# Attention scores as one burst of 64-row matmuls a block, two heads at once in the halves of the array, in a shared ring of four PSUM banks, with q unpadded and new costs in the planner

## The chip, the cores and the metric

One core of a Trainium2 chip. The metric is the device time of one execution in microseconds (us). Times of a kernel are medians of its executions; an execution counts as slow when it is over 1.5% above the fastest of its kernel, and the ratios leave it out. They are computed as said under the result. TensorE is PE, VectorE DVE, ScalarE ACT, GpSimd POOL, SyncE SP.

## The reference

Sliding-window attention with linear distance biases over 8 x 8 heads of 576 tokens, then a two-layer block with a squared ReLU:

```python
B, H, S, D = 8, 8, 576, 64
scores = (q @ k.T) / sqrt(D) - slope[h] * |i - j|      # only where 0 <= i - j < 128
attn   = softmax(scores)
x      = (attn @ v) as [B*S, H*D]                      # 4608 x 512
h      = x @ w_in                                      # 512 x 2048
out    = relu(h)**2 @ w_out                            # 2048 x 512
```

## The kernel before

Everything is planned at build time: each piece of work is a task with an estimated cost on its engine, a due date (`key`), and slots of rings that it takes and gives back. A list scheduler walks through them, always takes the task that can start first, and so fixes the order of every engine's instructions. The estimates are not times of the chip; if they are wrong, the order is wrong, and an engine in its fixed order stands and waits (below, PE for 1.54 us at a score and DVE for 4.31 us at a copy).

A sequence is five blocks of tokens (four of 128, one of 64), so there are 40 blocks. For each block the kernel needs q and k transposed, the scores for this block and the one before it (two "parts"), the exponential on ACT, the mask on DVE, pv, the normalisation on DVE, and the result transposed into `xT`. From the third sequence on, transposes are DMAs on SP's queue. The large matmuls of 512 columns ("h" and "o") fill PE in between; group g of h needs xT of 512 tokens.

```python
plan = Plan({"h": 2, "o": 2, "s": 2, "att": 2, ...})       # PSUM banks by ring
due = (b * S + kb * 128 + n) / 4 - 192 - 150               # in large matmuls
...
# from the third sequence on:
t_k = plan.add({"SP": 100.0}, due - 80, turn_k, ..., dma=500.0)    # DMA transpose of k
t_t = plan.add({"SP": 100.0}, due - 80, turn_q, ..., dma=500.0)    # of q
for c2 in range(2):                                        # DVE: spread q's two heads,
    nc.vector.tensor_copy(qp[po:po + 64, :, c2, 0:n],      # the other half of the rows
                          qT[po:po + 64, :, 0:n])          # is zero
...
for c in range(4):                                         # two heads a matmul
    for part, mk in parts:                                 # 128 rows, 2n columns
        nc.tensor.matmul(slot_s[:, :, part, 0:n], kT[mk][:, c, :],
                         qp[:, c, :, 0:n], start=True, stop=True)
    # each c: its own bank, own exponential (ACT) and mask (DVE)
```

The softmax here doesn't subtract the row's maximum and nothing guards it: scores larger than these inputs give would overflow.

## Time and profile before

| | before |
|---|---|
| median of runs | 333.6 to 334.7 us in the sets below |
| span of the profile | 333.0 us |
| first large matmul (h) | 27.08 us |
| PE busy | 308.0 us, 92% |
| score matmuls | 288, all 128 x 128 |

The waits of PE in the middle stall are these two and five shorter ones (from PE's timeline; in brackets the idle time before the row and what ended it):

```profile
88.89 0.39 PE L364 MATMUL ps_s<-qp_92,kT_88 128*128 128x256 bf16 x2 [1.54 <-DMA kT_88<-kn_74]
102.09 0.28 PE L364 MATMUL ps_s<-qp_92,kT_86 128*128 128x256 bf16 x1 [1.53 <-DVE qp_92 L320]
```

The five others end at transposes of k too; the second one shown ends at DVE's copy of q, which had itself waited 1.66 us for the transpose of q. One thing about reading the lines: records are lost. The page counts 554 of 576 matmuls of h and 560 of 576 of o. A lost record leaves a hole of exactly one matmul (0.216 us). Where I sum holes from starts below, holes of that size after 27 us are left out as lost records. For the kernel before, the sum gives 13.3 us before 27 us, 2.5 between 27 and 57, 0.4 between 57 and 83, 7.3 between 83 and 126, and nothing after that.

### The profile page before, as it was taken

How to read it: one execution, taken by the hardware profiler on the slowest of the kernel's cores; microseconds unless marked ns; L12 is line 12 of the kernel's file. 1: busy time of each engine (PE TensorE's matmuls, PEld its weight loads, DVE VectorE, ACT ScalarE, POOL GpSimd, SP SyncE). 2: the span in 40 equal slices, each digit the busy share in tenths (PEclk: the TensorE clock that was granted, in tenths of full speed). 3: DMA queues.
4: the chain of work that ended last, by engine and by line, in shares of the span. 5: the costliest groups of instructions: out<-in, count | busy, mean ns of one | idle time of the engine just before them, and what ended most of it. 6: DMA issues, size and time to landing. Idle time of an engine off the chain costs nothing.

```text
span 333.0 us, 5942 instructions
## 1 busy us (share of the span) xinstructions
PE 308.0 (92%) x2098; PEld 164.8 (49%) x2136; DVE 182.3 (55%) x570; ACT 186.2 (56%) x362; POOL 107.4 (32%) x133
## 2 busy tenths in 40 slices
PE   1679999999887899999999999999999999999995
PEld 1555566446454555555555555555554444444442
DVE  6676797349676776665666655755554222222200
ACT  4595785558575565656565566655574344443411
POOL 8976757153473555363422521100000000000000
PEclk9999999999999999999999999999999999999999
DMA  9999999999999999999999999653112001000021
GB/s 73 140 200 168 171 199 149 161 148 143 133 180 160 165 177 214 163 181 181 169 130 115 139 157 117 100 89 66 47 50 56 31 33 61 34 33 31 31 94 63
DMA packets 169373, 39.58 MB, mean 119 GB/s; under 512 B 160640, under 2 KB 164736, under 8 KB 169344
## 3 DMA queue, kind: packets, MB, share of 16 engines
q0 software_dynamic: 116736, 18.36, 89.0%
q1 hardware_dynamic: 52608, 20.85, 34.0%
q8 instruction: 16, 0.26, 0.3%
q14 instruction: 13, 0.11, 0.1%
HBM read 36.70 MB, written 9.44 MB: 139 GB/s over the span
## 4 chain that ended last, share of the span: by engine, by line
PE 79%; DMA 9%; DVE 5%; ACT 4%; issue 1%; ACTq 0%
PE o L511 34%; PE h L482 33%; PE ps_s L364 7%; DMA kT_87<-kn_73 5%; DMA kT_85<-kn_71 4%; PE pv L405 4%; PE tp L332 1%; DVE P_95 L390 1%; ACT masks L221 1%; ACT qp_93 L293 1%; ACT P_97 L382 1%; PE xp L450 0%; ACT P_95 L382 0%; DVE g L496 0%; DVE x_100 L431 0%
## 5 line engine op out<-in xcount | busy, mean ns | idle before, releaser
L482 PE MATMUL h<-xT,w_in_sb 128*128 128x512 bf16 x554 | 152.6, 379 | 0.8
L511 PE MATMUL o<-w_out_sb,g 128*128 128x512 bf16 x560 | 151.7, 379 | 0.8
L490 ACT ACTIVATE rt<-h 128x512 bf16<-128x512 f32 x144 | 85.6, 597 | 83.9 <-PE h L482 78.5
L496 DVE TENSOR_TENSOR g<-rt 128x512 bf16<-128x512 bf16 x144 | 60.4, 420 | 70.3 <-ACT rt L490 68.9
L511 PEld LDWEIGHTS <-g 128*128 128x128 bf16 x576 | 54.6, 98 | 52.2
L482 PEld LDWEIGHTS <-w_in_sb 128*128 128x128 bf16 x576 | 54.8, 98 | 49.7 <-issue 0.2
L382 ACT ACTIVATE P_95<-ps_s 128x512 bf16<-128x512 f32 (+1 forms) x56 | 27.0, 507 | 12.4 <-PE ps_s L364 12.1
L522 ACT ACTIVATE osb<-o 128x512 f32<-128x512 f32 x36 | 21.5, 598 | 19.8 <-PE o L511 16.6
L382 ACT ACTIVATE P_96<-ps_s 128x512 bf16<-128x512 f32 (+1 forms) x52 | 25.9, 517 | 10.5 <-PE ps_s L364 10.0
L382 ACT ACTIVATE P_97<-ps_s 128x512 bf16<-128x512 f32 (+1 forms) x52 | 25.7, 516 | 7.3 <-PE ps_s L364 7.1
L390 DVE TENSOR_TENSOR P_95<-P_95,masks 128x512 bf16<-128x512 bf16 (+1 forms) x56 | 20.1, 364 | 13.5 <-ACT P_95 L382 12.8
L390 DVE TENSOR_TENSOR P_96<-P_96,masks 128x512 bf16<-128x512 bf16 (+1 forms) x52 | 18.9, 368 | 10.3 <-ACT P_96 L382 9.4
L426 DVE RECIPROCAL rec<-pv 128x4 f32<-128x4 f32 (+1 forms) x80 | 13.8, 176 | 16.7 <-PE pv L405 16.3
L390 DVE TENSOR_TENSOR P_97<-P_97,masks 128x512 bf16<-128x512 bf16 (+1 forms) x52 | 18.8, 367 | 7.3 <-ACT P_97 L382 6.6
L273 POOL DMA_DIRECT2D kn_74<-in_k_dram x10 | 8.5, 845 | 25.2 <-DMA kT_88<-kn_74 8.7
L273 POOL DMA_DIRECT2D kn_73<-in_k_dram x10 | 8.5, 847 | 22.9 <-DMA kT_87<-kn_73 21.1
L405 PEld LDWEIGHTS <-P_95 128*128 128x128 bf16 x200 | 10.2, 99 | 5.1 <-DVE P_95 L390 0.3
L364 PEld LDWEIGHTS <-kT_88 128*128 128x128 bf16 x72 | 6.9, 98 | 11.0 <-DMA kT_88<-kn_74 3.0
L364 PEld LDWEIGHTS <-kT_86 128*128 128x128 bf16 x72 | 7.1, 99 | 10.4 <-issue 2.6
L431 DVE TENSOR_TENSOR x_98<-pv,rec 128x256 bf16<-128x256 f32 (+1 forms) x28 | 11.7, 418 | 0.4
L273 POOL DMA_DIRECT2D qn_77<-in_q_dram x10 | 8.5, 847 | 10.1 <-DMA qT_89<-qn_77 3.8
L364 PEld LDWEIGHTS <-kT_85 128*128 128x128 bf16 x72 | 7.2, 101 | 8.7 <-issue 1.6
(107 smaller groups left out, 327.9 us busy)
## 6 DMA issues: line engine op xcount, KB each, us to landing
out_dram<-osb SPq DMA_DIRECT2D x36, 256.0 KB, 2.3
w_in_sb<-in_moe_w_in_dram POOLq DMA_DIRECT2D x4, 512.0 KB, 8.9
w_out_sb<-in_moe_w_out_dram POOLq DMA_DIRECT2D x4, 512.0 KB, 10.5
kn_71<-in_k_dram POOLq DMA_DIRECT2D x8, 128.0 KB, 6.4
qn_75<-in_q_dram POOLq DMA_DIRECT2D x8, 128.0 KB, 6.3
kn_72<-in_k_dram POOLq DMA_DIRECT2D x8, 128.0 KB, 7.4
qn_76<-in_q_dram POOLq DMA_DIRECT2D x8, 128.0 KB, 7.8
kn_73<-in_k_dram POOLq DMA_DIRECT2D x8, 128.0 KB, 6.5
```

What stands on the lines that cost most here:

```text
L273: nc.gpsimd.dma_start(o, src[b, :, kb * 128:kb * 128 + n, :].rearrange("h s d -> s h d"))
L364: nc.tensor.matmul(slot_s.tile.rearrange("p (c t q) -> p c t q", c=2, t=2)[:, :, part, 0:n], kT[sk_of[mk].idx][:, c, :], qp[sq.idx][:, c, ...
L382: nc.scalar.activation(view(Pt[sP.idx][:, 2 * c:2 * c + 2]), view(slot_s.tile.rearrange("p (c t q) -> p c t q", c=2, t=2)), AF.Exp, bias=0 ...
L390: nc.vector.tensor_tensor(pt, pt, view(masks[:, 2 * c:2 * c + 2]), op=ALU.mult)
L405: nc.tensor.matmul(slot_v.tile[:, hi * (D + 1):(hi + 1) * (D + 1)], Pt[sP.idx][:, h, part, :], vt[s_in[mk, "v"].idx][:, h, :], start=part ...
L426: nc.vector.reciprocal(srec.tile[0:n, :], pv[0:n, :, D])
L431: nc.vector.tensor_tensor(xt[sx.idx][0:n, hf * 256:(hf + 1) * 256].rearrange("p (h e) -> p h e", h=4), pv[0:n, :, 0:D], srec.tile[0:n, :]. ...
L482: nc.tensor.matmul(slot.tile, w_in_sb[:, cc, fc * 128:(fc + 1) * 128], xT[:, cc, g * 512:(g + 1) * 512], start=cc == 0, stop=cc == C - 1)
L490: nc.scalar.activation(srt.tile, slot.tile, AF.Relu, bias=0.0, scale=1.0)
L496: nc.vector.tensor_tensor(sg.tile[:, fc, :], srt.tile, srt.tile, op=ALU.mult)
L511: nc.tensor.matmul(slot.tile, sg.tile[:, fc, t * 128:(t + 1) * 128], w_out_sb[:, fc, :], start=fc == 0, stop=fc == FCB - 1)
L522: nc.scalar.activation(so.tile, slot.tile, AF.Copy)
```

## The change

It means to halve PE's work on scores. The heads are 64 wide, so a matmul for one head uses only 64 of the array's 128 rows (the trace of the changed kernel notes 64*128 for it, that of the kernel before 128*128 throughout). Before, q was padded with zeros so that one matmul of 128 rows did two heads in 256 columns. Now two matmuls of 64 rows, one in each half of the array, are to run at the same time. All scores of a block are one burst, to pay for the change of tiling mode once (0.19 us there and back, by the trace below). The program writes a burst into four banks of 512 columns, which come from one ring that pv and the PE transposes share from the second sequence on. The planner's numbers change too.

```diff
-    plan = Plan({"h": 2, "o": 2, "s": 2, "att": 2, "rec": 4, "rt": 3, "g": 2, "osb": 3, **size})
+    plan = Plan({"h": 2, "o": 2, "a": 4, "rec": 4, "rt": 3, "g": 2, "osb": 3, **size})
 ...
-    t_zero = plan.add({"DVE": 2000.0}, -9e5, zero)          # memsets of the padding
 ...
-        due = (b * S + kb * 128 + n) / 4 - 192 - 150
+        due = (b * S + kb * 128 + n) / 4 - 192 - 40
 ...
-            t_k = plan.add({"SP": 100.0}, due - 80, turn_k, ..., dma=500.0)
+            t_k = plan.add({"SP": 1280.0}, due - 80, turn_k, ..., dma=650.0)
 ...                                                         # turn_q and turn_x alike
-            for c2 in range(2):
-                def spread_q(c2=c2): ...                     # the DVE copies are gone
 ...
-        for c in range(C):
-            slot_s = Slot("s")
-            ...one matmul of 128 rows and 2n columns for each part
+        slot_s = [Slot("a") for _ in range(4)]
+        def burst():
+            for c in range(C):
+                for part, mk in parts:
+                    for half in range(2):
+                        rows = slice(half * 64, half * 64 + 64)
+                        nc.tensor.matmul(
+                            slot_s[2 * (c // 2) + half]...[:, c % 2, part, 0:n],
+                            kT[sk_of[mk].idx][rows, c, :], qT[sq.idx][rows, c, 0:n], ...)
 ...
-            plan.add({"SP": 100.0}, key, store, [te], [], [so])
+            plan.add({"SP": 350.0}, key, store, [te], [], [so])
```

(Cut: the planner's count of several slots of one ring, the places of heads in the mask, the rings of pv and of the transposes in the first sequence, slightly moved due dates of exponentials and masks, and q's single evacuation in the first two sequences.)

More of the change, by code (lines that the diff above doesn't have):

```diff
@@ L74, in avail @@
             at = t.ready
+            more = {}
             for s in t.acq:
@@ L79, in avail @@
                 n = self.bufs[s.tag]
-                if len(u) >= n:
-                    old = u[len(u) - n]
+                more[s.tag] = more.get(s.tag, 0) + 1
+                i = len(u) + more[s.tag] - 1 - n
+                if i >= 0:
+                    old = u[i]
                     if old.left:
@@ L171, in ring @@
         return [const.tile(shape, BF16, name=f"{name}_{i}") for i in range(n)]
-    size = {"kn": 4, "qn": 4, "v": 6, "kT": 4, "qT": 3, "qp": 3, "P": 3, "x": 3}
+    size = {"kn": 4, "qn": 4, "v": 6, "kT": 4, "qT": 3, "P": 3, "x": 3}
     kn = ring("kn", size["kn"], [128, d_model])
@@ L180 @@
     qT = ring("qT", size["qT"], [128, C, 128])
-    qp = ring("qp", size["qp"], [128, C, 2, 128])
     Pt = ring("P", size["P"], [128, H, 2, 128])
     xt = ring("x", size["x"], [128, d_model])
-    plan = Plan({"h": 2, "o": 2, "s": 2, "att": 2, "rec": 4, "rt": 3, "g": 2, "osb": 3, **size})
+    plan = Plan({"h": 2, "o": 2, "a": 4, "rec": 4, "rt": 3, "g": 2, "osb": 3, **size})
     def act(n):
@@ L217, with place @@
     t_mask = []
+    def place(h):
+        c, half = divmod(h, 2)
+        return 4 * (c // 2) + 2 * half + c % 2
     for h in range(H):
         def build_mask(h=h):
-            nc.scalar.activation(masks[:, h], dist, AF.Exp, bias=0.0,
+            nc.scalar.activation(masks[:, place(h)], dist, AF.Exp, bias=0.0,
                                  scale=-(2.0 ** (-8.0 * (h + 1) / H)))
         t_mask.append(plan.add({"ACT": act(256)}, -9e5 + h, build_mask, [t_dist]))
-    def zero():
-        for t in qp:
-            nc.vector.memset(t[0:64, :, 1, :], 0.0)
-            nc.vector.memset(t[64:128, :, 0, :], 0.0)
-    t_zero = plan.add({"DVE": 2000.0}, -9e5, zero)
     def ones():
@@ L297, in attention @@
         n = blk[kb]
-        due = (b * S + kb * 128 + n) / 4 - 192 - 150
+        due = (b * S + kb * 128 + n) / 4 - 192 - 40
         first = b == 0
         by_dma = b > 1
-        sk, sq = Slot("kT"), Slot("qp")
+        sk, sq = Slot("kT"), Slot("qT")
         sk_of[m] = sk
@@ L307, in attention @@
         if by_dma:
-            st = Slot("qT")
             def turn_k():
                 nc.sync.dma_start_transpose(kT[sk.idx], kn[s_in[m, "k"].idx])
-            t_k = plan.add({"SP": 100.0}, due - 80, turn_k, [t_in[m, "k"]], [sk], [s_in[m, "k"]], dma=500.0)
+            t_k = plan.add({"SP": 1280.0}, due - 80, turn_k, [t_in[m, "k"]], [sk], [s_in[m, "k"]], dma=650.0)
             def turn_q():
-                nc.sync.dma_start_transpose(qT[st.idx], qn[s_in[m, "q"].idx])
-            t_t = plan.add({"SP": 100.0}, due - 80, turn_q, [t_in[m, "q"]], [st], [s_in[m, "q"]], dma=500.0)
-            for c2 in range(2):
-                def spread_q(c2=c2):
-                    po = c2 * 64
-                    nc.vector.tensor_copy(qp[sq.idx][po:po + 64, :, c2, 0:n], qT[st.idx][po:po + 64, :, 0:n])
-                t_q.append(plan.add({"DVE": dve(C * n, 4)}, due - 56, spread_q, [t_t, t_zero],
-                                    [sq], [st]))
+                nc.sync.dma_start_transpose(qT[sq.idx], qn[s_in[m, "q"].idx])
+            t_q.append(plan.add({"SP": 1280.0}, due - 80, turn_q, [t_in[m, "q"]], [sq], [s_in[m, "q"]], dma=650.0))
         else:
-            slot = Slot("h" if first else "att")
+            slot = Slot("h" if first else "a")
             last = None
@@ L330, in emit @@
                     if i == 0:
-                        slot.tile = psum.tile([128, 1024], BF16, tag=slot.tag, name="tp")
+                        slot.tile = psum.tile([128, 1024], BF16, tag=slot.tag, bufs=plan.bufs[slot.tag], name="tp")
                     nc.tensor.transpose(slot.tile[:, i * 128:(i + 1) * 128], src[:, (i % C) * 128:(i % C + 1) * 128],
@@ L341, in attention, with evac_q @@
             t_k = plan.add(both if first else {"DVE": both["DVE"]}, due - 56, evac_k, [last], [], [slot])
-            for c2 in range(2):
-                def evac_q(c2=c2):
-                    po = c2 * 64
-                    o = qp[sq.idx][po:po + 64, :, c2, 0:n]
-                    i_ = slot.tile[po:po + 64, 512:1024].rearrange("p (c s) -> p c s", c=C)[:, :, 0:n]
-                    copy(t_q[c2], o, i_)
-                t_q.append(plan.add(both if first else {"ACT": both["ACT"]} if c2 else {"DVE": both["DVE"]},
-                                    due - 56, evac_q, [last, t_zero], [], [slot]))
+            def evac_q():
+                copy(t_q[0], qT[sq.idx][:, :, 0:n],
+                     slot.tile[:, 512:1024].rearrange("p (c s) -> p c s", c=C)[:, :, 0:n])
+            t_q.append(plan.add(both if first else {"ACT": both["ACT"]}, due - 56, evac_q, [last], [], [slot]))
         t_k_of[m] = t_k
@@ L356, in attention @@
         p0 = parts[0][0]
-        for c in range(C):
-            slot_s = Slot("s")
-            tm = None
-            for part, mk in parts:
-                def emit(c=c, slot_s=slot_s, part=part, mk=mk):
-                    if part == p0:
-                        slot_s.tile = psum.tile([128, 512], FP32, tag="s", name="ps_s")
-                    nc.tensor.matmul(
-                        slot_s.tile.rearrange("p (c t q) -> p c t q", c=2, t=2)[:, :, part, 0:n],
-                        kT[sk_of[mk].idx][:, c, :], qp[sq.idx][:, c, :, 0:n], start=True, stop=True)
-                rel = []
-                if c == C - 1:
-                    if part == 0 or kb == NKB - 1:
-                        rel.append(sk_of[mk])
-                    if part == 1:
-                        rel.append(sq)
-                tm = plan.add({"PE": mm(2 * n)}, due - 32 + 3 * c, emit,
-                              [tm, t_k_of[mk]] + t_q + (chain["s"] if tm is None else []),
-                              ([slot_s] + ([sP] if c == 0 else [])) if part == p0 else [], rel)
-            chain["s"] = [tm]
+        slot_s = [Slot("a") for _ in range(4)]
@@ new lines, in burst @@
+        def burst():
+            for sl in slot_s:
+                sl.tile = psum.tile([128, 512], FP32, tag="a", bufs=4, name="ps_s")
+            for c in range(C):
[3 more added lines that the diff above has]
+                        nc.tensor.matmul(
+                            slot_s[2 * (c // 2) + half].tile.rearrange("p (c t q) -> p c t q", c=2, t=2)[
+                                :, c % 2, part, 0:n],
+                            kT[sk_of[mk].idx][rows, c, :], qT[sq.idx][rows, c, 0:n], start=True, stop=True)
@@ L378, in view, with expo @@
+        rel = [sq] + [sk_of[mk] for part, mk in parts if part == 0 or kb == NKB - 1]
+        tm = plan.add({"PE": 220.0 + C * len(parts) * (max(n, 64) / 2.4 + 4)}, due - 28, burst,
+                      [t_k_of[mk] for _, mk in parts] + t_q + chain["s"], slot_s + [sP], rel)
+        chain["s"] = [tm]
+        for i in range(4):
             def view(t):
                 return t[:, :, p0:2, 0:n]
-            def expo(c=c, slot_s=slot_s):
-                nc.scalar.activation(view(Pt[sP.idx][:, 2 * c:2 * c + 2]),
-                                     view(slot_s.tile.rearrange("p (c t q) -> p c t q", c=2, t=2)),
+            def expo(i=i):
+                nc.scalar.activation(view(Pt[sP.idx][:, 2 * i:2 * i + 2]),
+                                     view(slot_s[i].tile.rearrange("p (c t q) -> p c t q", c=2, t=2)),
@@ L384, in expo @@
                                      AF.Exp, bias=0.0, scale=scale)
             cols = 2 * n * len(parts)
-            te = plan.add({"ACT": act(cols)}, due - 32 + 3 * c, expo, [tm], [], [slot_s])
-            def mask(c=c):
-                pt = view(Pt[sP.idx][:, 2 * c:2 * c + 2])
-                nc.vector.tensor_tensor(pt, pt, view(masks[:, 2 * c:2 * c + 2]), op=ALU.mult)
-            t_P.append(plan.add({"DVE": dve(cols, 2)}, due - 32 + 3 * c, mask, [te] + t_mask))
+            te = plan.add({"ACT": act(cols)}, due - 28 + 3 * i, expo, [tm], [], [slot_s[i]])
@@ L394, in attention, with mask @@
+            def mask(i=i):
+                pt = view(Pt[sP.idx][:, 2 * i:2 * i + 2])
+                nc.vector.tensor_tensor(pt, pt, view(masks[:, 2 * i:2 * i + 2]), op=ALU.mult)
+            t_P.append(plan.add({"DVE": dve(cols, 2)}, due - 28 + 3 * i, mask, [te] + t_mask))
         sx = Slot("x")
@@ L396, in attention @@
         for hf in range(2):
-            slot_v = Slot("att")
+            slot_v = Slot("o" if first else "a")
             last = None
@@ L403, in emit @@
                         if hi == 0 and part == p0:
-                            slot_v.tile = psum.tile([128, 512], FP32, tag="att", name="pv")
+                            slot_v.tile = psum.tile([128, 512], FP32, tag=slot_v.tag, bufs=plan.bufs[slot_v.tag], name="pv")
                         nc.tensor.matmul(
                             slot_v.tile[:, hi * (D + 1):(hi + 1) * (D + 1)],
-                            Pt[sP.idx][:, h, part, :], vt[s_in[mk, "v"].idx][:, h, :],
+                            Pt[sP.idx][:, place(h), part, :], vt[s_in[mk, "v"].idx][:, h, :],
                             start=part == p0, stop=part == 1)
@@ L416, in attention @@
                     last = plan.add({"PE": mm(D + 1)}, due - 12 + 4 * hf, emit,
-                                    [last, t_P[h // 2], t_in[mk, "v"]]
+                                    [last, t_P[place(h) // 2], t_in[mk, "v"]]
                                     + (t_P[2 * hf:2 * hf + 2] + chain["pv"] if new else []),
@@ L441, in turn_x @@
                 nc.sync.dma_start_transpose(xT[:, :, t0:t0 + n], xt[sx.idx][0:n, :])
-            t_xT[b, kb] = plan.add({"SP": 100.0}, due, turn_x, t_norm, [], [sx], dma=500.0)
+            t_xT[b, kb] = plan.add({"SP": 1280.0}, due, turn_x, t_norm, [], [sx], dma=650.0)
         else:
-            slot_x = Slot("o" if first else "att")
+            slot_x = Slot("h" if first else "a")
             last = None
@@ L448, in emit @@
                     if c == 0:
-                        slot_x.tile = psum.tile([128, 1024], BF16, tag=slot_x.tag, name="xp")
+                        slot_x.tile = psum.tile([128, 1024], BF16, tag=slot_x.tag, bufs=plan.bufs[slot_x.tag], name="xp")
                     nc.tensor.transpose(slot_x.tile[:, c * 128:(c + 1) * 128],
```

## The prediction

> **What bounds the kernel now.** I read the page first, then a table of busy time by stretches that I cut where the character of the run changes, then the instructions of TensorE (PE) and of the DMA queue (SP) in order of time. On the page, the busy shares, the PE row of the 40 slices and the chain that ended last:
>
> ```profile
> PE 308.0 (92%) x2098; PEld 164.8 (49%) x2136; DVE 182.3 (55%) x570; ACT 186.2 (56%) x362; POOL 107.4 (32%) x133
> ...
> PE   1679999999887899999999999999999999999995
> ...
> PE 79%; DMA 9%; DVE 5%; ACT 4%; issue 1%; ACTq 0%
> ```
>
> PE bounds the kernel: 79% of the chain, no other engine over 56%. But the row shows two weak places: the first four slices, and slices 11 to 14 (digits 8, 8, 7, 8). Nine per cent of the chain is DMA, so a transfer ends waits there. The stretches, with columns us, PE, PE's weight loads, DVE, ACT, POOL:
>
> ```profile
> 0.00:27.00 27.00, 14.83 (x164) 11.19 (x165) 18.96 (x68) 17.16 (x37) 22.30 (x31) 1.00 1.51 143
> 27.00:57.00 30.00, 28.45 (x252) 17.25 (x257) 22.92 (x75) 21.03 (x42) 20.98 (x27) 1.00 1.98 171
> ...
> 83.00:126.00 43.00, 36.84 (x306) 20.86 (x311) 30.85 (x106) 25.38 (x54) 21.71 (x27) 1.00 2.28 162
> ...
> 140.00:257.00 117.00, 116.22 (x787) 61.62 (x801) 69.75 (x212) 68.10 (x133) 26.39 (x32) 1.00 1.10 115
> 257.00:314.00 57.00, 56.69 (x259) 25.80 (x264) 14.04 (x33) 24.48 (x41) 0.00 (x0) 1.00 0.10 37
> ```
>
> PE is idle 12.2 us in the first 27, 1.6 us in the next 30, 6.2 us between 83 and 126, and 0.8 us in the 117 us after 140. So there are three regimes: a start set by the chain of the first five blocks through ACT and DVE, a middle that waits for something, and a long stretch where only PE's own work counts. What the middle waits for is in the DMA queue's own timeline (start, us, then the issue):
>
> ```profile
> 97.99 1.53 SPq L311 DMA_TRANSPOSE kT_87<-kn_73  x1
> 99.61 1.30 SPq L315 DMA_TRANSPOSE qT_89<-qn_78  x1
> 101.00 1.27 SPq L441 DMA_TRANSPOSE xT<-x_98  x1
> 102.38 1.74 SPq L311 DMA_TRANSPOSE kT_88<-kn_74  x1
> 104.20 1.81 SPq L315 DMA_TRANSPOSE qT_90<-qn_75  x1
> 106.10 1.23 SPq L441 DMA_TRANSPOSE xT<-x_99  x1
> 107.44 1.72 SPq L311 DMA_TRANSPOSE kT_85<-kn_71  x1
> ```
>
> Each transpose occupies the queue 1.2 to 1.8 us, and it is full: three per block and part of a store make about 4.7 us per block (kT issued at 97.99, 102.38 and 107.44). The scheduler of the kernel before believes that an issue costs 0.1 us. Its order of PE therefore puts only about 11 large matmuls between two blocks of attention here (2.4 us and some 2 us of attention work), faster than the queue can supply, and PE stands at the scores for kT, which lands some 7 us after its issue.
>
> The costs on PE, from its timeline in the dense stretch:
>
> ```profile
> 152.15 0.59 PE L482 MATMUL h<-xT,w_in_sb 128*128 128x512 bf16 x2
> 152.58 0.27 PE L364 MATMUL ps_s<-qp_94,kT_86 128*128 128x256 bf16 x1
> 152.69 0.27 PE L364 MATMUL ps_s<-qp_94,kT_87 128*128 128x256 bf16 x1
> ...
> 173.43 0.22 PE L364 MATMUL ps_s<-qp_94,kT_85 128*128 128x128 bf16 x1
> 173.49 0.22 PE L364 MATMUL ps_s<-qp_94,kT_86 128*128 128x128 bf16 x1
> 173.55 0.60 PE L482 MATMUL h<-xT,w_in_sb 128*128 128x512 bf16 x2
> ```
>
> Starts, not durations, give the pace: 0.216 us for 512 columns, 0.109 for 256, 0.057 for 128. A matmul of 512 columns lasts 0.38 us, so about 0.16 us of it is pipeline that the next one hides.
>
> [...] The trace before [...] does give 0.16 us as the size of a drain and 0.098 us for a weight load. [...]
>
> **The change part by part.**
> Scores. Before, 288 matmuls: 224 of 256 columns and 64 of 128 columns, 224 x 0.109 + 64 x 0.057 = 28.1 us of PE. After, 576 of half height and half width, in 40 bursts that the built order shows whole (S16 or, in the first block of a sequence, S8). If two halves run together, a full burst is 8 pairs x 0.057 = 0.46 us against 0.87. But it begins and ends with a change of mode. The order puts both changes next to large matmuls, so nothing hides them: I estimate 0.3 us for the two together (between one drain of 0.16, and two drains and two weight loads, 0.52). Full burst 0.76, gain 0.11 x 24 = 2.7 us. The 16 small bursts (first block, and last block of 64 rows) are 0.23 + 0.3 = 0.53 against 0.44, a loss of 1.5 us. Sum: -1.2 us, far from the 13 us that halving the work would suggest.
>
> q without padding. It removes 60 DVE copies (about 0.33 us for 128 rows, 0.24 for 64: some 19 us of DVE), the six memsets of 0.27 us, and one of two evacuations of q in each of the first ten blocks. DVE is 55% busy, so after 140 us this is worth nothing. At the start it is: the masks wait 4.15 us for DVE at 6.18, and ACT then does masks, exponentials and evacuations in one chain (exponentials of the five blocks begin at 8.6, 12.8, 17.5, 22.4 and 24.4). Against that, a burst waits for all four banks, so exponentials of one block no longer overlap scores of the next. One block is then about 0.9 us of burst, 0.2 latency and 4 x 0.54 of exponentials, 3.4 us, with at most one 0.6 us evacuation between; before it was 3.9 to 4.7. I expect the first large matmul at 25 instead of 27.1: -2 us.
>
> Order. The planner now counts 1.28 us for a transpose, and attention gets a later due date (40 in place of 150). By the built order, blocks 10 to 19 start their scores at large matmuls 138, 155, 175, 195, 214, 230, 247, 268, 300, 326, where before they were at 159, 166, 173, 179, 187, 198, 209, 221, 230, 250. So about 20 large matmuls a block, 4.3 us, and about 1.9 of attention: 6.2 us a block, slower than the 4.7 that the queue can do. The 6.2 us idle of 83 to 126 should go, with the short gaps inside: -6.5 us.
> The price: attention ends later. Before, the last pv of a block stood 82 to 160 large matmuls ahead of the first h that needs its tokens, from group 3 on; now 33 to 50, for group 2 it is 29. The norm and xT's landing (2.4 to 8 us) take up to 9 us, against 29 x 0.216 = 6.3 us and a burst. I add +1 us for that.
>
> Sum: 334.3 - 1.2 - 2 - 6.5 + 1 = 325.6; I say 326.
>
> **The rivals.**
> First: the halves don't run together, or each weight load waits for its own half. Then a full burst is 16 x 0.057 + 0.3 = 1.2 us and a small one 0.8: +0.34 x 24 + 0.32 x 16 = +13 us, about 340 in all. For it: nothing in the trace shows tiles. Against it: [...] weight loads that keep up with pv at one each 0.03 us.
> Second: changes of mode cost little (0.2 us), the bursts save 5 us and the time is near 322.
> Third: the shared ring of four banks becomes the wait. A burst needs both pv banks normed by DVE. By the order, 12 large matmuls (2.6 us) stand between the last pv and the next burst, and DVE needs about 1.2 us for both halves; the exponentials, 4 x 0.54 and two relus, fit the 16 (3.5 us) before pv narrowly. In the first ten blocks, where transposes use the ring too, it is tighter. I give it +3 us at most: 329.
> Fourth: the stall is not the queue but the loads (DMA busy in every slice until 220 us). Then it only moves, and the time is about 331. Against it: the queue is gapless there, and PE waits for transposes, not for loads.
>
> **Range and chances.** 326, from 319 (cheap mode changes, no new waits) to 334 (dear changes, ring waits, half of the stall kept). The 2% line is 327.6, close to my value: faster 0.56, same 0.36, slower 0.08, the last being mainly the first rival.
>
> **What would show it.** In PE's timeline, starts within a burst in pairs a few ns apart and 0.057 us from pair to pair, with a hole of about 0.15 us on each side; a burst from large matmul to large matmul 0.7 to 0.85 us. First h near 25 us. In the DMA queue, gaps between transposes after 80 us; PE idle under 2 us in the stretch where blocks 10 to 19 run. In the waits, no PE ps_s for a DMA. DVE busy near 160 us. I am wrong if starts in a burst are 0.057 us apart one by one, if PE waits at bursts for DVE's norm, or if h waits for xT at the start of a group.

## The result

323.68 us against 333.62 us, medians of four runs each; ratio 0.9703, 95% interval 0.9607 to 0.9798. A ratio is the mean time of one kernel's fast runs over that of the other's of the same rounds, so it isn't quite the ratio of the medians. It is faster. The time lies inside the range and 2.3 us below the value.

The page of the changed kernel, the same rows as before:

```profile
PE 305.3 (94%) x2424; PEld 153.9 (47%) x2424; DVE 168.9 (52%) x498; ACT 178.6 (55%) x358; POOL 107.5 (33%) x133
...
PE   2789999999879999999999999999999999999995
PEclk9999999999979999999999999999999999999999
...
PE 89%; DMA 4%; DVE 2%; ACT 2%; POOL 1%; issue 1%; POOLq 0%; ACTq 0%
```

PE's share of the chain rose from 79% to 89%. The four weak slices of the middle became two (an 8 and a 7), and in the second of them the granted clock dips to 7. The stretches, with the same columns as before:

```profile
0.00:27.00 27.00, 16.87 (x212) 12.31 (x213) 17.34 (x64) 15.18 (x35) 21.70 (x31) 1.00 1.51 142
...
83.00:126.00 43.00, 39.52 (x338) 19.61 (x337) 24.52 (x74) 23.16 (x49) 18.86 (x23) 0.96 1.75 160
...
140.00:257.00 117.00, 117.00 (x932) 57.39 (x931) 66.07 (x187) 68.66 (x138) 30.95 (x38) 1.00 1.14 120
```

Between 83 and 126 us PE is idle 3.5 us, not 6.2, and everywhere after that not at all. What a burst costs is in PE's timeline:

```profile
149.70 0.59 PE L469 MATMUL h<-xT,w_in_sb 128*128 128x512 bf16 x2
150.22 0.23 PE L356 MATMUL ps_s<-qT_91,kT_87 64*128 64x128 bf16 x2
150.29 0.22 PE L356 MATMUL ps_s<-qT_91,kT_88 64*128 64x128 bf16 x2
...
150.63 0.22 PE L356 MATMUL ps_s<-qT_91,kT_88 64*128 64x128 bf16 x2
150.78 1.47 PE L498 MATMUL o<-w_out_sb,g 128*128 128x512 bf16 x6
```

Each row "x2" is a pair, whose two starts lie 3 to 4 ns apart in the trace; pairs follow each other every 0.056 us. The halves do run together: a pair takes the 0.056 us that in the trace before lies between the starts of two single matmuls of 128 columns. The last h should free PE at 150.13 (two times 0.216 after 149.70); the first pair starts 0.095 us later. The last pair should take 0.056 us and o starts 0.148 after it, so the hole at the end is 0.09. What happens in the two holes isn't shown. Changing the mode there and back costs 0.19 us, and the whole burst 0.65 us. A little more comes after it: the next large matmul starts 0.226 us after the first one behind a burst, not 0.216, so 0.20 us in all.

The one wait left in the middle is this (PE's timeline):

```profile
86.75 0.82 PE L498 MATMUL o<-w_out_sb,g 128*128 128x512 bf16 x3
91.05 1.87 PE L469 MATMUL h<-xT,w_in_sb 128*128 128x512 bf16 x4 [3.48 <-DMA xT<-x_95]
```

It is h of group 2. xT was issued at 81.98 us and landed 9.03 us later. After the wait, four large matmuls take 1.87 us: 0.43 us from start to start, twice the usual. A table by short stretches shows the granted clock (the third number from the end):

```profile
87.00:91.00 4.00, 0.57 (x3) 0.17 (x2) 1.12 (x4) 0.95 (x4) 1.76 (x3) 0.99 1.84 125
91.00:92.00 1.00, 0.95 (x3) 0.39 (x3) 0.00 (x0) 0.00 (x0) 0.00 (x0) 0.50 1.60 171
```

So a hole of 3.64 us is followed by 3.4 us at half clock (the trace records 0.50 from 90.92 to 94.33 us). (The longest hole after 27 us without half clock behind it, in any trace here, is 2.1 us, in the kernel before with the issue costs only; what lies between isn't shown.) With the slow matmuls, holes sum to 5.3 us in this stretch: the wait costs some 1.7 us again after it has ended.

### The profile page after: what moved, and what is told of

Its sections match the earlier page's. It is cut to its first block, busy times and chain, and to the rows that moved or that the text cites.

```text
span 324.1 us, 6468 instructions
## 1 busy us (share of the span) xinstructions
PE 305.3 (94%) x2424; PEld 153.9 (47%) x2424; DVE 168.9 (52%) x498; ACT 178.6 (55%) x358; POOL 107.5 (33%) x133
## 4 chain that ended last, share of the span: by engine, by line
PE 89%; DMA 4%; DVE 2%; ACT 2%; POOL 1%; issue 1%; POOLq 0%; ACTq 0%
PE h L469 38%; PE o L498 38%; PE ps_s L356 6%; PE pv L392 5%; DMA xT<-x_95 3%; PE tp L324 1%; DMA qn_76<-in_q_dram 1%; PE xp L437 1%; ACT rt L477 1%; DVE P_92 L377 0%; ACT qT_91 L293 0%; POOL kn_71 L273 0%; POOL vt_79 L273 0%; POOL qn_75 L273 0%; DVE kT_86 L291 0%
## 5 line engine op out<-in xcount | busy, mean ns | idle before, releaser
L469 PE MATMUL h<-xT,w_in_sb 128*128 128x512 bf16 x576 | 147.6, 382 | 4.3 <-DMA xT<-x_95 3.5
L498 PE MATMUL o<-w_out_sb,g 128*128 128x512 bf16 x576 | 148.3, 379 | 0.0
L469 PEld LDWEIGHTS <-w_in_sb 128*128 128x128 bf16 x576 | 53.9, 98 | 63.2 <-issue 5.7
L498 PEld LDWEIGHTS <-g 128*128 128x128 bf16 x576 | 51.6, 98 | 54.6
L369 ACT ACTIVATE P_94<-ps_s 128x512 bf16<-128x512 f32 (+1 forms) x52 | 22.9, 524 | 5.0 <-PE ps_s L356 5.0
L369 ACT ACTIVATE P_92<-ps_s 128x512 bf16<-128x512 f32 (+1 forms) x56 | 24.2, 513 | 2.2 <-PE ps_s L356 2.1
L369 ACT ACTIVATE P_93<-ps_s 128x512 bf16<-128x512 f32 (+1 forms) x52 | 23.0, 523 | 2.2 <-PE ps_s L356 2.1
L273 POOL DMA_DIRECT2D kn_74<-in_k_dram x10 | 8.5, 848 | 20.5 <-DMA kT_88<-kn_74 18.4
L273 POOL DMA_DIRECT2D kn_73<-in_k_dram x10 | 8.5, 848 | 20.2 <-DMA kT_87<-kn_73 19.3
L273 POOL DMA_DIRECT2D kn_71<-in_k_dram x10 | 8.7, 866 | 15.6 <-DMA kT_85<-kn_71 11.7
L392 PEld LDWEIGHTS <-P_92 128*128 128x128 bf16 x200 | 9.8, 99 | 6.8 <-DVE P_92 L377 1.4
L273 POOL DMA_DIRECT2D kn_72<-in_k_dram x10 | 8.5, 850 | 13.6 <-DMA kT_86<-kn_72 13.0
L392 PEld LDWEIGHTS <-P_94 128*128 128x128 bf16 x184 | 9.5, 102 | 6.3 <-issue 0.8
L392 PEld LDWEIGHTS <-P_93 128*128 128x128 bf16 x192 | 9.5, 100 | 5.9 <-DVE P_93 L377 0.5
```

The lines of the kernel that those rows point to most:

```text
L273: nc.gpsimd.dma_start(o, src[b, :, kb * 128:kb * 128 + n, :].rearrange("h s d -> s h d"))
L369: nc.scalar.activation(view(Pt[sP.idx][:, 2 * i:2 * i + 2]), view(slot_s[i].tile.rearrange("p (c t q) -> p c t q", c=2, t=2)), AF.Exp, bia ...
L392: nc.tensor.matmul(slot_v.tile[:, hi * (D + 1):(hi + 1) * (D + 1)], Pt[sP.idx][:, place(h), part, :], vt[s_in[mk, "v"].idx][:, h, :], star ...
L469: nc.tensor.matmul(slot.tile, w_in_sb[:, cc, fc * 128:(fc + 1) * 128], xT[:, cc, g * 512:(g + 1) * 512], start=cc == 0, stop=cc == C - 1)
L498: nc.tensor.matmul(slot.tile, sg.tile[:, fc, t * 128:(t + 1) * 128], w_out_sb[:, fc, :], start=fc == 0, stop=fc == FCB - 1)
```

## The experiments

Twelve kernels. Each set shares runs of the kernel before; the sets' medians of before were 333.90, 334.68 and 333.75 us. The first set is the yardstick, both numbers, the old numbers and full height; the second is the halves one after the other, two bursts, all work of the padding and xT 5 us later; the third is the rest. The record gives each set another chip number. Where I say "more than the changed kernel", the yardstick's 322.47 is meant, also across sets; "by the ratios" stands for the difference of the two ratios times 334 us.

Four runs count as slow: one of the yardstick (its profiled one), one of the issue costs only (333.56), one of two bursts (337.08), and one of before in the second set (338.94). Medians and ranges below contain them, ratios don't; without them the medians are 322.33, 330.96, 332.04 and 334.56. The yardstick's slow run is 1.6% above its fastest and had the wait at group 2, so its ratio leaves out a run with the very wait in question.

| what was run | median us | lowest to highest | ratio to before, 95% interval |
|---|---|---|---|
| changed kernel again | 322.47 | 321.34 to 326.54 | 0.9656, 0.9626 to 0.9685 |
| before + both planner numbers | 328.04 | 327.47 to 328.89 | 0.9834, 0.9804 to 0.9864 |
| before + issue costs only | 331.08 | 328.56 to 333.56 | 0.9891, 0.9848 to 0.9934 |
| before + due dates only | 330.18 | 329.23 to 331.12 | 0.9882, 0.9850 to 0.9915 |
| changed, planner's old numbers | 322.45 | 320.99 to 323.84 | 0.9667, 0.9635 to 0.9700 |
| changed, full-height scores | 326.70 | 325.28 to 327.20 | 0.9786, 0.9758 to 0.9814 |
| changed, halves one after the other | 328.98 | 327.70 to 330.22 | 0.9837, 0.9807 to 0.9866 |
| changed, two bursts a block | 332.09 | 331.03 to 337.08 | 0.9925, 0.9901 to 0.9950 |
| changed + all work of the padding | 329.07 | 326.70 to 331.06 | 0.9835, 0.9787 to 0.9883 |
| changed + DVE copies only | 325.23 | 323.95 to 325.75 | 0.9728, 0.9696 to 0.9760 |
| changed, xT planned 5 us later | 320.79 | 320.55 to 322.20 | 0.9605, 0.9578 to 0.9633 |
| changed, xT 7 us later, earlier dates | 321.46 | 320.97 to 323.20 | 0.9629, 0.9596 to 0.9663 |

**The yardstick.** No edit.

> The changed kernel once more, as the yardstick of this set. 323.7 us, with a spread from 321 to 326 us that depends on whether h of token group 2 waits for a landing of xT (3.6 us in the profile, followed by about 3 us at half clock). If the spread has another cause, the fast runs will not show a shorter wait.

Measured: 322.47 us. The profiled run was 326.54 us, and its trace again has the hole before h of group 2, now 3.95 us, with xT landing 7.9 us after its issue. The other runs, of which no trace exists, lay between 321.3 and 322.7. The granted clock: of the nine runs of this kernel, with the result's, 321.15 and 321.34 had 1.000, four of 322.2 to 322.7 had 0.995, and three of 325.1 to 326.5 had 0.992 to 0.994; the two with a trace, and the wait, are of the last group. A clock of 0.995 can come without the wait: the changed kernel with the planner's old numbers (below) ran its profiled execution at 0.995, with half clock between 24.5 and 27.9 us, behind no hole over 1.2 us. So the spread has two parts, the wait and the clock.

**Was it the planner's numbers that removed the stall?** The kernel before, with the numbers alone:

```diff
-        due = (b * S + kb * 128 + n) / 4 - 192 - 150
+        due = (b * S + kb * 128 + n) / 4 - 192 - 40
-  {"SP": 100.0} ... dma=500.0      # transposes; stores 100.0
+  {"SP": 1280.0} ... dma=650.0     # transposes; stores 350.0
```

> The kernel before with only the planner's new numbers (1.28 us for an issue of a transpose, 0.35 us for a store, due dates 110 large matmuls later); scores and q untouched. Theory A, that of the prediction: these numbers slow attention down to what the DMA queue can supply, so 6 of the 6.5 us come back: 327 to 328 us, PE idle under 2 us in the stretch of blocks 10 to 19. Theory B: the slower pace comes from the burst that needs all four banks, not from the numbers; the built order of this kernel still has the scores of blocks 10 to 14 only 7 to 9 large matmuls apart. Then at least two thirds of the stall stay there: 331 to 334 us.

Measured: 328.04 us, 5.5 us less by the ratio, and the row for 83 to 126 us, which before had 36.84 busy:

```profile
83.00:126.00 43.00, 43.00 (x318) 23.27 (x317) 29.82 (x97) 26.45 (x55) 23.53 (x28) 1.00 1.84 177
```

PE never stands. Theory A holds for the old kernel, and my argument for theory B was wrong: I had looked at the spacing of blocks 10 to 14, but the rings let the queue run some blocks ahead, so these blocks find their transposes landed. The first wait of the stall is at block 15, counted from 0 (at 88.89 us), and there this order leaves room (blocks 14 to 17 at large matmuls 190, 219, 243, 264 in place of 187, 198, 209, 221). The two numbers one at a time:

> The kernel before with only the planner's cost of a DMA issue corrected (1.28 us for a transpose, 0.35 us for a store); due dates as before. Both numbers together gave 328.0 us against 333.9 and no idle PE after 57 us. If the cost of an issue is what mattered, this gives at least 4 of those 6 us (327.5 to 330 us) and the queue shows gaps; if the due date did, it stays at 332 to 334 us.

> The kernel before with only the due dates moved, an issue still counted as 0.1 us. In its built order the blocks up to 15 are as tight as before (starts at large matmuls 179, 187, 198, 212) and from block 17 on they are 16 to 52 apart. The stall of the kernel before begins at block 14, so I expect 2 to 3 us of idle PE to stay at blocks 14 to 16 and the rest to go: 329 to 331 us. If only the issue cost matters: 333 us.

Measured: 331.08 and 330.18 us, with 2.8 and 2.3 us of holes left between 83 and 257 us by starts, of 7.3. The issue costs alone came out at the slow end and gained less than the 4 us expected. Either removes most of the stall, and only both remove all of it. What is left differs: with the issue costs alone PE waits for DVE's copies of q, 2.1 us at block 19; with the due dates alone 1.4 of the 2.3 us are h waiting for xT, 0.8 the scores of blocks 15 and 16. Now the reverse, the changed kernel with the planner's old numbers:

```diff
-        due = (b * S + kb * 128 + n) / 4 - 192 - 40
+        due = (b * S + kb * 128 + n) / 4 - 192 - 150
-  {"SP": 1280.0} ... dma=650.0     # stores 350.0
+  {"SP": 100.0} ... dma=500.0      # stores 100.0
```

> The changed kernel with the planner's old numbers (0.1 us for an issue, 0.5 us for a transfer, due dates 150 ahead). Theory A: the stall of the kernel before comes back, about 329 us. Theory B: the four-bank ring keeps blocks 10 to 19 at 15 to 20 large matmuls apart (the built order says so), so there is no such stall: 321 to 325 us. Either way h of group 2 has a lead of 26 large matmuls in place of 29, so its wait for xT should be 0.5 us longer or so.

Measured: 322.45 us, the same as the changed kernel, and for 83 to 126 us:

```profile
83.00:126.00 43.00, 43.00 (x402) 21.68 (x400) 29.84 (x92) 28.28 (x61) 22.11 (x27) 1.00 1.98 176
```

So in the changed kernel the numbers are not needed. The form of the scores does it as well: with the old numbers the built order still starts blocks 10 to 13 at large matmuls 137, 154, 174, 194, where the kernel before had 159, 166, 173, 179. A burst that takes all four banks can't be planned before the last block's pv has been normalised, so the planner itself spreads blocks. That the ring is what spreads them is an inference from the built orders; no run changes the ring alone. Nor does one put DVE's copies of q back under the old numbers, so their absence may have a part: one of the seven waits of the stall ended at such a copy. One expectation failed: h of group 2 has three large matmuls less of lead here and didn't wait at all, because xT landed 4.65 us after its issue in place of 9.03.

**What are the tiles worth?** The changed kernel, each pair replaced by one matmul of full height. It sums two heads. Its output is wrong, which doesn't matter for the time. (The comparison can't see this error at these inputs.)

```diff
-                    for half in range(2):
-                        rows = slice(half * 64, half * 64 + 64)
-                        nc.tensor.matmul(..., kT[..][rows, c, :], qT[..][rows, c, 0:n], ...)
+                    nc.tensor.matmul(slot_s[c]..., kT[..][:, c, :],
+                                     qT[..][:, c, 0:n].unsqueeze(1).to_broadcast([128, 2, n]), ...)
```

> The changed kernel with each pair of half-height matmuls replaced by one matmul of full height and 256 columns that reads q twice (wrong results on purpose: two heads are summed); order, ring, banks and everything else as in the changed kernel. If the halves and the changes of mode cost on the path what the trace shows (0.648 us for a full burst, 0.425 to 0.435 for a small one, against 0.87 and 0.44 to 0.46), this is 24 x 0.22 + 16 x 0.02 = 5.6 us slower than the changed kernel, about 329 us. The rival, that the gain comes from the order alone: within 2 us of the changed kernel.

Measured: 326.70 us, 4.2 more than the changed kernel, where 5.6 was expected. A burst in its timeline:

```profile
148.85 1.04 PE L354 MATMUL ps_s<-qT,kT 128*128 128x256 bf16 x8
149.73 1.46 PE L496 MATMUL o<-w_out_sb,g 128*128 128x512 bf16 x6
```

From start to start that is 0.88 us, against 0.65. Its PE reaches group 2 later, and xT didn't keep it waiting there: it has no holes at all between 57 and 257 us. So the fairer comparison is with the changed kernel without the wait (320.79, below, from another set): 5.9 us, where the sum over bursts says 5.6. The tiles are worth about what the trace of a burst says, and it lies on the path.

**Do neighbours have to lie in different halves?**

```diff
-            for c in range(C):
-                for part, mk in parts:
-                    for half in range(2):
+            for half in range(2):
+                for c in range(C):
+                    for part, mk in parts:
```

> The changed kernel with one loop moved: in each burst all matmuls of the upper half first, then all of the lower half, so neighbours no longer lie in different halves. Same count, same banks, same order otherwise. If matmuls run together only because neighbours lie in different halves, a full burst becomes 16 x 0.057 + 0.19 = 1.1 us in place of 0.65 and the kernel is about 24 x 0.45 + 16 x 0.23 = 14 us slower, near 337 us. If the array runs any two of its halves together whatever their distance, nothing changes.

Measured: 328.98 us, 6.5 more than the changed kernel where 14 was expected, and neither theory. (Its trace has no wait for xT; against the version without that wait, of the same set, it is 8.2. Its bursts give 6.9, and its first large matmul comes at 26.16 us, 1.2 later.) A full burst takes 0.89 us, not 1.1. The 16 starts of the burst at 186.14 us form two series, each with a pitch of 0.056 us: one from 186.136 to 186.538, the other from 186.378 to 186.779. The series are the halves: no record names its half, but the first matmul on each bank carries a semaphore wait. By the program these are the 1st, 5th, 9th and 13th of a burst; in order of time they stand 1st, 5th, 6th and 13th in 28 of the 32 bursts of 16. The second series begins when five matmuls of the first have started, and they overlap from there on. So matmuls of one half queue behind each other, and those of the other half go round them, here three of them; what limits this isn't shown. Alternating halves is what fills both from the start (0.65 us a burst, against 0.89).

**What does a change of mode cost?** Two bursts of two banks in each block, with separate rings as before:

```diff
-    plan = Plan({"h": 2, "o": 2, "a": 4, ...
+    plan = Plan({"h": 2, "o": 2, "s": 2, "att": 2, ...
-        slot_s = [Slot("a") for _ in range(4)]      # one burst, c in range(4)
+        slot_s = [Slot("s") for _ in range(4)]
+        for j in range(2): ...                      # burst j: c in range(2*j, 2*j + 2)
```

> The changed kernel with two bursts of two banks in each block, with separate rings for scores (2 banks) and the rest (2 banks) as in the kernel before: twice the changes of tiling mode. If a pair of changes costs 0.19 us wherever it stands beside large matmuls, 40 more pairs cost 7.6 us, less some 1 us where they fall into idle time at the start: 328 to 330 us. If the cost is one of the burst's length, or hidden, within 2 us of the changed kernel. A wait for xT at group 2 (lead of 25 large matmuls) may add up to 4 us.

Measured: 332.09 us, 9.6 more than the changed kernel (9.0 by the ratios) and 2 above what was expected. A half burst of a full block:

```profile
153.10 1.03 PE L471 MATMUL h<-xT,w_in_sb 128*128 128x512 bf16 x4
154.06 0.40 PE L356 MATMUL ps_s<-qT,kT 64*128 64x128 bf16 x8
154.39 1.47 PE L500 MATMUL o<-w_out_sb,g 128*128 128x512 bf16 x6
```

h frees PE at 153.97 (four times 0.216 after 153.10), and o starts at 154.39: 0.42 us. Two of them make 0.85 us for a full block, where one burst costs 0.65. So a pair of mode changes costs 0.19 us here too, and 40 more of them are 7.6 us by this sum; the run doesn't part them from the rest. The rest is in other places: the first large matmul starts at 27.7 us in place of 25.1, the clock was half between 26.1 and 32.9 us, and h of group 2 again waited, 1.55 us.

**Does it matter that q is no longer padded?** The changed kernel, with all the work of the padding put back, though nothing reads the padded q. The burst waits for it as before.

```diff
+    t_zero = plan.add({"DVE": 2000.0}, -9e5, zero)                  # memsets of qp
 ...
-            def evac_q(): copy(t_q[0], qT[...][:, :, 0:n], ...)     # first ten blocks
+            for c2 in range(2):                                     # each half of the rows
+                def evac_q(c2=c2): copy(t_q[c2], qT[...][po:po + 64, :, 0:n], ...)
 ...
+            for c2 in range(2):                                     # all later blocks
+                def spread_q(c2=c2):
+                    nc.vector.tensor_copy(qp[...][po:po + 64, :, c2, 0:n], qT[...][po:po + 64, :, 0:n])
```

> The changed kernel with the work of the padding put back but not used by the scores (right results): six memsets, two evacuations of q in place of one in the first ten blocks, two DVE copies of q for each later block, which the burst waits for. If the padding cost only the start, the first large matmul comes 1 to 2 us later than at 25.1 us and nothing else changes: 324 to 325 us. Rival: DVE's 19 us of copies count in the long stretch too; then more than 3 us.

Measured: 329.07 us, 6.6 more than the changed kernel (6.0 by the ratios). The expectation is missed, and the rival was right that the copies count. The first large matmul starts at 28.21 us, 3.1 later (in this trace large matmuls still start 0.42 us apart at 29 us, as at half clock; whether the clock has a part in the delay isn't shown). The first copy runs at 69.87 us, and after it PE has holes again: by starts 1.6 us between 83 and 126, and 2.5 between 126 and 257, where the changed kernel has, but for the wait at group 2, none and 0.2. The longest of the late ones, 1.53 us at 204.2, ends at a pv that waited for the mask of P. DVE's timeline at this place:

```profile
204.33 0.86 DVE L326 COPY qp<-qT 64x512 bf16<-64x512 bf16 x2 [4.31 <-DMA qT<-qn]
205.22 0.43 DVE L501 TENSOR_TENSOR g<-rt 128x512 bf16<-128x512 bf16 x1
205.57 0.89 DVE L395 TENSOR_TENSOR P<-P,masks 128x256 bf16<-128x256 bf16 x4
```

In the brackets are the idle time before the row and what ended it: DVE stood for 4.31 us because the copy, next in its order, waited for a transpose to land. The masks behind it were not let past: they start at 205.57 us, the copies at 204.33. So it is not DVE's busy time that costs, but a wait put into an engine's fixed order. To part this from the start, the copies alone, without memsets and second evacuations (the first two hunks are left out):

```diff
+            for c2 in range(2):                                     # blocks from the third sequence on
+                def spread_q(c2=c2): nc.vector.tensor_copy(qp[...], qT[...])
```

> The changed kernel with only the two DVE copies of q for each block from the eleventh on put back, which the burst waits for; no memsets, and one evacuation of q in the first ten blocks. The kernel with all of the padding's work was 6.5 us slower than the changed kernel: first large matmul at 28.2 in place of 25.1, and waits of pv for masks on DVE that stood behind a copy waiting for its DMA. If that split is right, the first large matmul is at 25.1 again and the copies alone cost 2 to 3 us: 324.5 to 325.5 us, with DVE waiting for the DMA of qT before such copies.

Measured: 325.23 us, 2.8 more than the changed kernel (2.4 by the ratios). The first large matmul starts at 25.16 us, so the start's 3 us belong to the memsets and evacuations. Holes by starts are 2.1, 1.1 and 1.2 us in 57 to 83, 83 to 126 and 126 to 257, 4.4 in all, of which 0.8 lie after 140 us. There is no wait for xT here, so the fairer comparison is again with the version without it: also 4.4 us. From this kernel's table of waits:

```profile
DVE qp L320 <- DMA qT<-qn: 18.4, 11, 3.7
```

DVE stood 18.4 us in eleven waits of this kind. Twice a burst on PE then stood in its middle, 1.7 us together (until 72.58 and 95.31 us), for a bank that DVE's norm (x) had not yet freed, because the norm stood behind such a copy. But the same copies cost nothing in the kernel before with both planner numbers: its table has no wait of DVE for a DMA at all, and PE has 0.02 us of holes after 83 us. The cost hangs on where the order puts a copy relative to its landing.

**Can the new wait be planned away?** The planner believes that a transpose has landed 0.9 us after its turn on the queue. For xT alone, it is told 5.9:

```diff
-                t.end = self.dma_free + 900.0
+                t.end = self.dma_free + 900.0 + (t.lat or 0.0)
 ...
-            t_xT[b, kb] = plan.add({"SP": 1280.0}, due, turn_x, ..., dma=650.0)
+            t_xT[b, kb] = plan.add({"SP": 1280.0}, due, turn_x, ..., lat=5000.0, dma=650.0)
```

> The changed kernel whose planner counts 5 us more until a transposed x has landed; nothing else. The built order then puts 48 large matmuls in place of 29 between the last pv that group 2 needs and its h. If the wait of 3.6 us at h and the half clock after it are what separates the slow runs of the changed kernel (325 to 326 us) from the fast ones (321), all runs lie at 320 to 321.5 us, with no wait for xT in the profile. Rival: the spread has another cause, and runs of 325 us stay.

Measured: 320.79 us, 3.95% less than before by the ratio. The built order now has 48 large matmuls between the last pv and h of group 2, in place of 29, and PE doesn't wait for xT anywhere, although this xT still landed 8.2 us after its issue. The row for 83 to 126 us:

```profile
83.00:126.00 43.00, 42.31 (x365) 21.41 (x371) 26.43 (x83) 26.91 (x57) 19.55 (x25) 1.00 1.93 168
```

The clock is 1.00, where the changed kernel had 0.96. This trace lost 41 of the 1152 large matmuls, so its busy time reads a little low: by starts, no hole over 0.1 us is left after 57 us but lost records. Two of its six runs, 322.06 and 322.20, lie outside the 320 to 321.5 that was expected; both had a granted clock of 0.995, the other four 1.000. It beats the kernel before clearly and the changed one narrowly: the intervals, 0.9578 to 0.9633 and 0.9626 to 0.9685, just touch. One more step, 7 us and due dates 40 large matmuls earlier:

```diff
-        due = (b * S + kb * 128 + n) / 4 - 192 - 40
+        due = (b * S + kb * 128 + n) / 4 - 192 - 80
-  lat=5000.0
+  lat=7000.0
```

> The changed kernel with 7 us more counted for the landing of a transposed x, and due dates 40 large matmuls earlier. Leads at the starts of groups are 55 to 89 large matmuls but for group 1. With 5 us and the old due dates it was 320.8 us, and only its start still had holes. So no more is to be had here: 320 to 321.5 us; if a second wait for xT had been hidden under the first, it is 1 us faster.

Measured: 321.46 us, no further gain, as expected. What is left of holes lies mostly in the start: some 11 us before the first large matmul. In this last kernel two bursts also waited for the transpose of q, 1.1 us together (at 92 and 111 us).

## Why the prediction was right or wrong

The range held, and the value was 2.3 us too high. The steps under it were less good than the sum. I take the two profiled spans, 333.04 and 324.07 us, 9.0 apart.

**Bursts: the mechanism was right, the size off.** The term that failed is "0.3 us for the two together". It measured 0.19 us, in the changed kernel and again with two bursts a block. A full burst takes 0.65 us, not 0.76, and a small one 0.43, not 0.53. Over all bursts, 24 x (0.872 - 0.648) + 8 x (0.436 - 0.425) + 8 x (0.456 - 0.435) = 5.6 us gained instead of 1.2. The run with full-height matmuls agrees: 5.9 us against the version without the wait. (With the 0.01 us that the matmul behind a burst loses, the sum is 5.2.) The estimate took the whole 0.16 us by which a matmul of 512 columns outlasts its pace in the trace before (0.379 us long, its end modelled, and 0.216 from start to start) as lost at a change, once or twice; that a change drains anything was assumed, and no trace shows it. Each change left a hole of only 0.095. The second rival came true, with its "saves 5 us". The first one didn't: the halves do run together, and issuing them one after the other, which takes a part of the overlap away, costs 6.5 us.

**Start: right.** First h at 25.07 us, where 25 was predicted. The runs that put the padding's work back show that the memsets and evacuations are worth 3 us there. That DVE is the only link in this chain isn't shown: evacuations went from ACT as well. One reading was off: by the starts that the prediction lists, blocks before lie 4.2, 4.7, 4.9 and 2.0 us apart, not 3.9 to 4.7.

**DVE after 140 us: the value right, the reason wrong.** The kernel before has no holes after 126 us, so there was nothing for the copies' removal to gain there. But "DVE is 55% busy, so after 140 us this is worth nothing" doesn't hold as a reason: put back into the changed kernel, the copies cost 2.8 to 4.4 us, most of it before 140 us, a stretch that the prediction gave no value for DVE, and 0.8 after it. The step that failed is reading an engine's busy share as freedom; what counted here is what stood behind a wait in DVE's fixed order (4.31 us at one copy, with the masks behind it). DVE's busy time itself fell to 168.9 us, where 160 was the forecast.

**The middle stall: size right, cause half right.** The stall is gone; it was 7.3 us by starts, and 6.5 was predicted. Transposes have gaps between them: kT is issued at 101.11, 106.64, 114.69 and 122.02 us, 7.0 us apart on average, the scores of blocks 10 to 19 start 6.1 us apart (6.2 predicted), and no score waits for a DMA. The planner's numbers are sufficient for that (5.5 us in the kernel before) but not needed (the changed kernel with the old numbers is as fast). The prediction put them down as what spreads the blocks; it missed that the new form of the scores does it too, by the built order through the burst of four banks. The fourth rival, the loads, is out: the stall vanished without any load being moved away.

**The price of late attention: right place, too small.** h of group 2 was named, with its lead of 29 large matmuls, and it is where PE waits. "I add +1 us" measured 5.3 in the profiled run, of which 3.6 is the wait and 1.7 the half clock after it. The estimate had up to 9 us for the norm and the landing together; the landing alone took 9.03, and the clock wasn't in it. In the median of runs it is less: 322.47 against 320.79 without the wait, about 1.7 us, and a part of that is the clock: runs at 1.000 are 321.15 and 321.34 against 320.55 to 320.80. What stays open is why an xT lands after 4.7 us in one kernel and 9.0 in another; no run isolates that.

**The ring as a new wait: not seen in the changed kernel.** The third rival expected PE to wait for DVE's norm at the bursts. No such wait is in the table of the changed kernel. But the rival isn't empty: with the copies put back, two bursts waited for the norm, 1.7 us together.

**The sum** for the profiled spans: start -2.0, bursts after the start -4.9 (21 full and 14 small ones), holes between 27 and 83 us -1.1, the old stall -7.3, the new wait +5.3, the rest +0.2: -9.8, where the spans say -9.0. So 0.8 us are unaccounted for; the slower matmul behind each of the 35 bursts is 0.4 of them. The good value is partly luck: bursts 4.4 us better than thought, and the wait 4.3 worse.

## What to carry to other kernels

Running two 64-row matmuls at once costs a change of mode there and back (0.19 us here), so gather them in one burst (0.65 us, where two half bursts took 0.85) and alternate the halves (0.89 us without that); measure one burst from the large matmul before to the one after. Work on an engine that isn't the bound is not free if it can stand ahead of something urgent in the engine's fixed order: with the copies put back, DVE stood 18.4 us in eleven waits for transposes, and the kernel took 2.8 us more. A planner needs the issue and the landing times that the trace shows (here, for k and q of 128 x 512 bf16 in the changed kernel: 1.2 us on SP's queue in the median and up to 2.9, and landings from 2.4 to 11.1 us after the issue); a lead that was a few us short cost twice here, because each of the two holes of 3.6 and 3.9 us was followed by 3.4 us of half clock.
